# Recurrent linear attention and an MLP mixer on one core: u of batches 2 and 3 transposed by DMA instead of TensorE

## The chip, the core and the metric

The kernel runs on one NeuronCore of a Trainium2 chip. The core has five engines with instruction streams of their own: TensorE (PE; its weight loads, PEld, are listed apart) multiplies matrices into PSUM, eight banks of 128 x 512 float32; VectorE (DVE) and ScalarE (ACT) read PSUM and SBUF; GpSimd (POOL) works on SBUF; SyncE (SP) here issues DMAs. Sixteen DMA engines move data between HBM and SBUF. The metric is the time of one execution in microseconds of device time. Lower is better.

## The reference

Four batches, 8 heads, 768 time steps, head size 48. First a recurrence with a decaying state, then a mixer over time steps and over channels:

```python
for t in range(S):                                    # S = 768
    state = alpha[:, :, t, :, None] * state + einsum('bhd,bhe->bhde', k[:, :, t], v[:, :, t])
    y[:, :, t] = einsum('bhd,bhde->bhe', q[:, :, t], state)
x = y.transpose(0, 2, 1, 3).reshape(B, S, H * D)      # 4 x 768 x 384
h = relu(x^T @ w_tok1) @ w_tok2                       # over time: 768 -> 256 -> 768
u = x + h^T
out = u + relu(u @ w_ch1) @ w_ch2                     # over channels: 384 -> 1536 -> 384
```

Inputs and output are float32; the kernel multiplies in bfloat16 and sums in float32.

## The kernel before

A batch is cut into six chunks of 128 time steps; unit n is batch n // 6, chunk n % 6. The work of a batch has these stages, named as the program names its operations:

- Loads: alpha, k, q and v of a chunk, 192 KB each, float32, by SyncE into `in` buffers with eight slots (line 205). Batch 0 and the start of batch 1 load pairs of chunks, 384 KB.
- Attention of a chunk: `la` is the logarithm of alpha (ScalarE), `cum` its running sum over the chunk (one matmul of 384 columns and four of one column, lines 352 and 355), `ek` and `eq` its exponentials (ScalarE), `pkk` and `pkq` k and q scaled by them (mostly GpSimd, line 275), `tr` and `tp` their transposes through PSUM, `gt` and `gm` the products of keys and queries and their mask, `state`, `st` and `ss` the carried state, `y` the result, copied to the tile x as bfloat16.
- Token mixing: `tok1` (line 602), `ht` (its relu), then `tok2`, two matmuls a chunk (line 651), and `u`, an addition on VectorE that turns the tile x of a chunk into u in place (line 657).
- Transposing u: the channel matmuls need u with channels on the partitions. In `separate` (batches 1 to 3), for each half of a batch (three chunks), operation `utp` transposes the three x tiles by 18 small matmuls against the identity, two 64-row halves of each of nine 128 x 128 blocks, into two PSUM banks (`row_tiles`, line 289), and two operations `ut` copy the banks to the tile `ut` (line 669), one a 64-row half. Batch 0 (`mixed`) computes u transposed directly and keeps doing so.
- Channel mixing (`channel`): 24 `ch1` of three matmuls a batch, reading `ut` (line 691), each followed by `rt`, a relu out of PSUM into one of 24 `rt` tiles (line 589 on ScalarE, 591 on VectorE); then for each chunk three `ch2` parts of four matmuls (line 715), `o` (adds u, line 728) and `out`, a store of 192 KB by SyncE (line 731).

Nothing is scheduled at run time. The functions above only build a list of operations; `ORDER`, a text found by an offline planner, says in which order they are emitted, and each engine runs its own instructions in that order. An entry is an operation's number in the list; digits after a point are the PSUM banks that it gets; a letter A, D or P chooses ScalarE, VectorE or GpSimd where there is a choice; `f` and a bank is a filler, a matmul of zeros (line 792), of which there are 61, all ahead of the first ch1 of batch 0. The numbers in `costs` and the new `late` are what the planner reckoned with, in microseconds; the program does not read them. An instruction that must wait holds up all that stand behind it on its engine; this holds for SyncE's and ScalarE's DMA issues too.

In the order before, u of batch 2 is transposed at 107.9 us and that of batch 3 at 144.9 us of the profiled execution, between the last ch2 parts of the batch before and the first ch1 of its own; the attention of batch 3 is spread among the ch1 of batch 2.

Of the kernel before, what the change touches and what calls it, by code (L numbers as in the profile page):

```python
# [17 lines left out]
FUSE = 99  # L18
FETCH, BLOCK, AHEAD, ARRIVES = 193, 256, 449, (4.5, 30.0, 3.0)
# [6 lines left out]
0 1 f0 2 f0 f0 f0 f0 f0 3 f0 f0 f0 f0 f0 4 28 f0 29 f0 f0 30.0 5 31.1 32 f2 f2 38 6 f2 35 f2 33 f2 f2 f2 39 f2 34 f2  # L26
36 40 f2 43.2 41 7 f3 66 47.3 f4 65 48 44 49A 50D f4 67.4 46A 45D 68.5 69 f6 51.67 75 72 54.01 8 70 52 f3 f3 76 f3 73
f3 77 f3 80.3 78 f2 9 84.2 56 f6 85 105 81 71 f6 104 87D f6 f6 10 86A f6 f6 83D 106.6 82A 55 107.5 108 53 91.14 11 114
88.23 92 f0 42P 37A f0 f0 109 90 f0 58.07 115 89 57.13 60A 93 f2 116 12 f2 f2 59 f2 f2 f2 112 f2 111 63 61 117 14
123.2 64A f0 62 f0 124 74A 79P 119.0 110 16 120 125D 126A f4 94.41 122A 121D 18 96 127.57 97 130.36 95.20 128 113A  # L30
118P 100 132 98 102 133.4 99A 20 131 13P f5 103A 169.5 101 163.6 24 166.2 f3 15P 129 141.3 135 142.0 143 136 134.17
17P 137 139 145 138D 147 140A 144 146 259 148 150 149 151 19D 152 172.4 178.1 162A 161D 175.7 f0 173 176 174A 167 177D
260 164 168A 170 22D 21P 165A 179 f0 171A 23D f0 261 f0 180A f0 189.0 201.3 190A 195.4 262 202A 181.7 27D 25P 196A
185.2 26D 182A 153 193.6 186A 211.5 264 194D 223.1 263 212D 227.0 224A 265.3 228A 266.4 155 267 217.7 273 270 207.2
274 209.6 268 300 208D 218A 276 213.5 210D 215.1 214A 269 187.0 301 271 216A 203.4 188A 219.3 275 204A 302 225.2 220A
154D 199.7 272 226A 278.65 277 279 200A 303 221.1 280D 281A 156P 183.0 222A 282 283 184A 292.43 284D 285A 197.2 304
294 286.71 157 305 198D 289.05 205.6 287 306.4 288 206A 159 191.2 308 291 307.7 309 311 239.6 296 314 343 290 315
249.1 297 192D 293.54 344 312 319.37 298 295A 345 254.0 316 299A 234.2 158A 346 317 244.5 347 310 313 160D 240 318 348
245 351 241 349 320 352.4 242A 321D 246 322A 354 235 247D 353 350 358 236 356 243 323 362 324 237D 333.64 357 325A
326D 376.5 238 363.2 335 250 248 355 364 336 486 365 327.37 251 487 329 366 367 330.62 328 252A 488 255 332 368 256  # L40
339 369 359.73 331 257A 370.12 340 229.4 361A 360D 253 372D 371A 377 373.60 258 510 334.73 375 489 381.21 341 490 374
337 230 342A 378 382 338A 491 379.5 383 231 380A 492 384.0 232D 511.6 385A 493 513 388.3 512 516 233 386.2 389A 514
517 494 521 495 515 387D 522.7 390.1 496 523 398.5 391 524 394.4 526 396.0 399 392.6 395 400.3 527 535.2 393 518.17
401 497 402.54 528 519A 397 529.63 525 403A 553.1 404D 498 520A 536 405.05 530A 416.4 499 554 406A 440.7 407D 555 531A
500 417D 420.2 539 434.6 421D 441A 501 532.10 435A 550.53 534 422.4 502 430.2 551 546 423A 540.7 533 431A 452.6 558
552 442.0 541 537.5 453D 503 542 438.4 544 538D 559.2 439A 556.1 443D 504 560 543 412.3 545 557D 561 426.6 413D 505
432.7 564 427A 410.5 506 433A 446.4 562 411A 565 408.0 507 447A 563 572.1 577 450.2 409D 508 454.3 573 451A 547.67 574
455D 566.54 509 548A 578.0 549D 591.1 568A 567D 448.2 720 592 580 424.3 584 449D 579 588.76 583 721 425A 569.54 590
418.1 596 582 436.2 570 419A 414.0 571 437A 581 597.3 593 589 722 610.6 575.5 598 444.1 415D 599 601 723 576A 594.2
611 445A 481.4 595D 602 724 744 428.7 476.0 600 429A 725 603 604.35 612 585.61 605A 726 466.2 587D 586A 477 727 606A  # L50
482 728 607.73 751 615.16 609 483 729 755 616 471.5 608 478 617 613.3 730 479 472 614A 484 618.1 480 762 456.7 619D
473 485 773 622.6 731 474 732 620.0 623A 475 457 621A 733 458 734 634.3 459 630.4 735 628.1 635 632.5 631 624.6 780
460 626.0 629 461.7 625 792 736 627 462 737 633 463 636.34 738 464 639.16 637A 467 638D 640A 641D 465 468 799 774.0
469 745.5 775 793.7 656.4 746 778 747 756.3 470 650.6 795 739 757 749 684.1 651D 740 758 644.2 685D 776 748 662.5 794
760 645D 741 660.6 811 663D 657A 678.3 750 742 661D 787.0 769.1 679A 812.7 770 759 668.2 743 777 813 761 672.5 788 814
664.4 669A 673D 789 670.6 665A 666.3 779 671A 646.1 830 667D 682.0 798 647A 831.7 683A 806.2 781.54 797 832 807 763.63
833 752.10 765D 658.2 783A 835 754D 764A 674.7 753D 659D 782A 686.3 808 675D 800.40 687A 803.16 796 802D 816 784.25
801A 766.73 804 680.0 768 818 654.4 681A 836 767 648.1 655A 844.3 786 642.0 649A 817 771.7 785 822.41 643A 652.5 772A
805 834 837 790.2 824 815 653A 809.0 791A 823 838.76 810A 819.51 825.2 839D 820A 828.4 840D 676.0 821A 826 715.7 829D
827 677A 849.65 841.21 845 716 843 846 700.4 851 695.0 850 696 842 852.3 688.1 853D 847.5 689A 705.6 848D 697 854.2  # L60
698 699 717 855A 710.3 718 711 701 719 702 856.1 703 704 712 857A 690.5 713 858.0 714 868.2 859 862.7 860.4 869 864.1
863 866.3 691 861 867 692 865 706 693 873.02 694 870.74 874A 875D 707 871D 872A 910.3 708 894.1 911A 709 880.5 895A
908.2 881D 906.0 909A 912.7 907A 900.4 913A 876.6 901A 896.3 877A 918.1 897A 914.5 919D 904.2 915A 922.0 905D 902.7
923D 920.4 903A 898.6 921A 916.3 899A 888.1 917A 890.5 889A 884.2 891D 878.0 885A 886.7 879A 882.4 887A 892.6 883D
929.3 893A 939.1 930 931 940 932 944.5 933 945 946 934.2 947 941 948 924.0 942 925 943 926 935 927 936 928 949.7 937
950 938 951 954.4 955 952 956 953 957 958
# [12 lines left out]
class Graph:  # L79
# [5 lines left out]
    def add(self, name, costs, emit, reads=(), writes=(), prio=0, dma=None, new=(), tail=0.0, rows=False, loose=False, n=0, late=0.0):  # L85
        self.ops.append(Op(costs, emit, new))
        return self.ops[-1]
# [6 lines left out]
def kernel(  # L94
# [12 lines left out]
    nc = tc.nc  # L107
    B, H, S, D = q.shape
    C = 128
# [232 lines left out]
    def natural_front(n):  # L342
# [7 lines left out]
        def cum(e):  # L350
# [3 lines left out]
            for j in range(4):  # L354
                pe.matmul(ps[:, HD + j : HD + j + 1], lhsT=la[:, 2 * j : 2 * j + 2, :], rhs=ones_col,  # L355
                          start=True, stop=True, skip_group_check=True)
# [478 lines left out]
```

## Time and profile before

| | |
|---|---|
| median of 3 runs | 174.6 us (173.99 to 174.98) |
| the profiled execution's own time | 174.24 us |
| its span, first to last instruction | 172.5 us |
| granted TensorE clock | 1.0 |
| TensorE busy | 166.5 us (96%) |
| TensorE weight loads | 106.8 us |
| VectorE, ScalarE, GpSimd busy | 102.0, 96.0, 72.3 us |
| DMA | 30.20 MB, 175 GB/s over the span |

The profile is of one execution. Its page has the busy time of each engine, the span in 40 slices (a digit is the busy share in tenths), the chain of work that ended last, and groups of instructions by source line. Further views of the trace are used below: the busy time in stretches of the span (length, then busy time and count of TensorE, its weight loads, VectorE, ScalarE and GpSimd, then the granted clock, the DMA engines' share and GB/s), the list of who waited for whom (total, times, longest), the chain of waits in order of time (start, length, instruction), the timeline of an engine, and the instructions of one source line (duration least, median and greatest in ns, first and last start). Matmuls overlap, so their pitch is read from the chain, where each entry begins at the end of the one before, and not from their durations. A DMA's time to landing runs from its issue to its semaphore.

### The profile page before, as it was taken

How to read it: one execution, taken by the hardware profiler on the slowest of the kernel's cores; microseconds unless marked ns; L12 is line 12 of the kernel's file. 1: busy time of each engine (PE TensorE's matmuls, PEld its weight loads, DVE VectorE, ACT ScalarE, POOL GpSimd, SP SyncE). 2: the span in 40 equal slices, each digit the busy share in tenths (PEclk: the TensorE clock that was granted, in tenths of full speed). 3: DMA queues.
4: the chain of work that ended last, by engine and by line, in shares of the span. 5: the costliest groups of instructions: out<-in, count | busy, mean ns of one | idle time of the engine just before them, and what ended most of it. 6: DMA issues, size and time to landing. Idle time of an engine off the chain costs nothing.

```text
span 172.5 us, 5143 instructions
## 1 busy us (share of the span) xinstructions
PE 166.5 (96%) x2099; PEld 106.8 (62%) x2099; DVE 102.0 (59%) x212; ACT 96.0 (56%) x206; POOL 72.3 (42%) x114
## 2 busy tenths in 40 slices
PE   7999979999999999999999999999999999999993
PEld 3566656665666567566666665666676656656562
DVE  3159977544653597689593727495988248132231
ACT  2577552699865655497887231699771112865000
POOL 7252542319485782944877111499941000000000
PEclk9999999999999999999999999999999999999999
DMA  5999999999998999999999999995000221100133
GB/s 134 261 261 265 232 335 398 309 234 337 256 307 168 205 254 219 225 170 198 165 204 151 196 219 223 211 210 92 4 4 0 79 104 50 46 4 0 46 115 113
DMA packets 86150, 30.20 MB, mean 175 GB/s; under 512 B 79600, under 2 KB 85104, under 8 KB 86128
## 3 DMA queue, kind: packets, MB, share of 16 engines
q1 hardware_dynamic: 86128, 29.89, 75.2%
q8 instruction: 16, 0.26, 0.7%
q14 instruction: 6, 0.05, 0.1%
HBM read 25.17 MB, written 4.72 MB: 173 GB/s over the span
## 4 chain that ended last, share of the span: by engine, by line
PE 78%; DVE 6%; POOL 4%; DMA 3%; issue 3%; ACT 2%; SPq 1%; DVEq 0%; POOLq 0%
PE bank L691 27%; PE bank L715 23%; PE bank L289 4%; PE bank L651 3%; DMA ina<-in_alpha_dram 3%; PE bank L602 3%; DVE gm L309 2%; PE bank L387 2%; PE bank L338 2%; PE bank L423 2%; POOL pkk L275 2%; PE bank L521 1%; PE bank L411 1%; PE bank L352 1%; SPq L205 1%
## 5 line engine op out<-in xcount | busy, mean ns | idle before, releaser
L691 PE MATMUL bank<-ut,wc 128*128 128x384 bf16 x288 | 51.1, 326 | 0.0
L691 PEld LDWEIGHTS <-wc 128*128 128x128 bf16 x288 | 26.6, 98 | 16.5
L275 POOL TENSOR_TENSOR pkk<-ink,ek 128x384 bf16<-128x384 f32 x24 | 24.3, 1022 | 17.7 <-ACT ek L256 14.9
L715 PE MATMUL bank<-wc,rt 128*128 128x384 bf16 x144 | 26.5, 326 | 0.0
L715 PE MATMUL bank<-wc,rt_late 128*128 128x384 bf16 (+2 forms) x156 | 25.1, 314 | 0.0
L728 DVE TENSOR_TENSOR o<-bank,x 128x384 f32<-128x384 f32 (+2 forms) x19 | 10.1, 536 | 18.2 <-PE bank L715 18.2
L589 ACT ACTIVATE rt<-bank 128x384 bf16<-128x384 f32 x33 | 16.3, 494 | 7.4 <-PE bank L691 7.0
L282 POOL CAST vb<-inv 128x384 bf16<-128x384 f32 x21 | 10.5, 506 | 22.3 <-DMA inv<-in_v_dram 17.6
L715 PEld LDWEIGHTS <-rt_late 128*128 128x128 bf16 x156 | 14.4, 98 | 8.2
L275 POOL TENSOR_TENSOR pkq<-inq,eq 128x384 bf16<-128x384 f32 x18 | 17.9, 1003 | 2.8 <-ACT eq L258 2.8
L589 ACT ACTIVATE rt_late<-bank 128x384 bf16<-128x384 f32 x33 | 16.1, 495 | 5.3 <-PE bank L691 5.3
L309 DVE TENSOR_TENSOR gm<-bank,u 128x512 bf16<-128x512 f32 x28 | 17.3, 682 | 2.8 <-PE bank L387 2.6
L243 ACT ACTIVATE la<-ina 128x384 bf16<-128x384 f32 x24 | 12.1, 526 | 10.8 <-DMA ina<-in_alpha_dram 10.8
L715 PEld LDWEIGHTS <-rt 128*128 128x128 bf16 x144 | 13.2, 98 | 7.7
L792 PE MATMUL bank<-zeros 128*128 128x384 bf16 x61 | 15.1, 372 | 1.4 <-DVE la L192 1.2
L591 DVE TENSOR_SCALAR rt_late<-bank 128x384 bf16<-128x384 f32 x15 | 8.3, 554 | 10.0 <-PE bank L691 8.3
L309 DVE TENSOR_TENSOR gm<-bank,pmask 128x512 bf16<-128x512 f32 x20 | 12.7, 682 | 1.4 <-PE bank L521 1.3
L256 ACT ACTIVATE ek<-bank 128x384 f32<-128x384 f32 x24 | 11.4, 498 | 3.5 <-PE bank L355 2.0
L333 ACT CAST x<-bank 128x384 bf16<-128x384 f32 x16 | 7.3, 483 | 10.6 <-PE bank L338 9.4
L322 POOL TENSOR_TENSOR ss<-st,al 128x384 bf16<-128x384 f32 x12 | 10.0, 832 | 7.4 <-DVE st L319 5.4
L591 DVE TENSOR_SCALAR rt<-bank 128x384 bf16<-128x384 f32 x15 | 7.9, 554 | 5.3 <-PE bank L691 5.3
L297 ACT COPY tkq<-bank 128x512 bf16<-128x512 bf16 x17 | 9.3, 602 | 2.8 <-PE bank L289 2.7
(118 smaller groups left out, 237.3 us busy)
## 6 DMA issues: line engine op xcount, KB each, us to landing
out_dram<-o SPq DMA_DIRECT2D x23, 192.0 KB, 2.6
ina<-in_alpha_dram SPq DMA_DIRECT2D x14, 192.0 KB, 4.3
ink<-in_k_dram SPq DMA_DIRECT2D x14, 192.0 KB, 4.6
inq<-in_q_dram SPq DMA_DIRECT2D x14, 192.0 KB, 4.5
inv<-in_v_dram SPq DMA_DIRECT2D x14, 192.0 KB, 4.4
rt_late<-in_moe_w_ch_dram SPq DMA_DIRECT2D x2, 1152.0 KB, 10.1
rt_late<-in_moe_w_ch_dram SPq DMA_DIRECT2D x4, 576.0 KB, 7.1
ina<-in_alpha_dram SPq DMA_DIRECT2D x5, 384.0 KB, 6.3
```

Of the source, the lines that this page charges most:

```text
L243: g.add("la", {"ACT": 0.43}, lambda e: act.activation(la[:, :, 0:D], t, AF.Ln), key, [u["la"][1]], pr + 5)
L256: g.add("ek", {"ACT": 0.38}, lambda e: act.activation(ek, banks[bank.place][:, 0:HD], AF.Exp, scale=-1.0), [bank], [kek], pr + 4)
L275: lambda e, dst=dst, src=src, ex=ex: {"POOL": gps, "DVE": dve}[e].tensor_tensor(dst[:, :, 0:D], src, ex().rearrange("p (h d) -> p h d", h= ...
L282: lambda e: evict[e](vb, src), ksrc, [u["vb"][1]], pr + 4)
L309: g.add("gm", {"DVE": 0.60}, lambda e: dve.tensor_tensor(gm, banks[bank.place].rearrange("p (j t) -> p j t", j=4), wide(mask, [[0, 4], lis ...
L322: g.add("ss", {"POOL": 0.79}, lambda e: gps.tensor_tensor(ss, st.rearrange("p (h d) -> p h d", h=H), wide(al, [[1, 8], [0, D]]), ALU.mult) ...
L589: act.activation(dst, src, AF.Relu)
L591: dve.tensor_scalar_max(dst, src, 0.0)
L691: pe.matmul(banks[bank.place][:, 0:HD], lhsT=wc1[wp][:, kc, off : off + 128], rhs=ut_t[b % 2][:, kc, cs], start=(kc == 0), stop=(kc == NM ...
L715: pe.matmul(banks[bank.place][:, 0 : hi - lo], lhsT=rt_t[(b * NDC + mc) % NRT][:, i * 128 : i * 128 + 128], rhs=wc2[:, mc, lo:hi], start=( ...
L728: g.add("o", {"DVE": 0.09 + 0.38 * width}, lambda e, i=i, bank=bank, o=o, lo=lo, hi=hi: dve.tensor_tensor(o[:, lo:hi], banks[bank.place][: ...
L792: pe.matmul(banks[place][:, 0:HD], lhsT=zeros[:, 0:128], rhs=zeros, start=True, stop=True, skip_group_check=True)
```

## The change

For batches 2 and 3 the 18 transposing matmuls and two copies of each half are replaced by one DMA that ScalarE issues, which reads three x tiles of 128 x 384 and writes them transposed from SBUF to SBUF. For this the x tiles become slices of four larger tiles of three chunks, and `ut` gets the layout chunk, channel block, time, so that one half is one contiguous run on each partition. The copies and matmuls that write and read `ut` are rewritten for the layout, with the same sizes. Batch 1 is transposed as before. The two other options that the diff brings, `TRD` and `TOT`, are off. The loads are the same transfers as before.

The operation list is eight shorter, so operations behind those of batch 2 have new numbers, and the whole order was searched anew with the costs of the diff: 1.3 us of ScalarE for a transposing DMA, and its data 3.0 us later. It has 63 fillers, again all ahead of the first ch1.

```diff
+UTD, TRD, TOT = (2, 3), (), False
...
-    x_t = many("x", NX, [128, HD])
+    x_all = many("x", 4, [128, 3, HD])
+    x_t = [x_all[n // 3][:, n % 3, :] for n in range(NX)]
...
-    ut_t = many("ut", 2, [128, NM, S])
+    ut_t = many("ut", 2, [128, NCH, NM, C])
...
             ku = [("x", (n0 + i) % NX) for i in mine]
+            if b in UTD:
+                x = x_all[(n0 + mine[0]) % NX // 3]
+                g.add("utd", {"ACT": 1.3}, lambda e, x=x, cs=cs: nc.scalar.dma_start_transpose(
+                    ut[:, cs].rearrange("p i j t -> p (i j) t"), x.rearrange("p i d -> p (i d)")), ku,
+                    [("ut", b % 2, j, part, h) for j in range(NM) for h in range(2)], 1000 * b + 170, late=3.0)
+                continue
             tb = [Bank(), Bank()]
...
             for h in range(2):
                 g.add("ut", {"ACT": 0.50, "DVE": 0.43}, lambda e, tb=tb, h=h, cs=cs: evict[e](
-                    ut[:, :, cs].rearrange("p j (i t) -> p j i t", t=128)[:, :, :, 64 * h : 64 * h + 64],
+                    ut[:, cs, :, 64 * h : 64 * h + 64].rearrange("p i j t -> p j i t"),
...
                 pe.matmul(banks[bank.place][:, 0:HD], lhsT=wc1[wp][:, kc, off : off + 128],
-                              rhs=ut_t[b % 2][:, kc, cs], start=(kc == 0), stop=(kc == NM - 1),
+                              rhs=ut_t[b % 2][:, ti, kc, :], start=(kc == 0), stop=(kc == NM - 1),
```

Of the two orders, the stretch in which u of batch 2 is transposed. Before:

```
460 626.0 629 461.7 625 792 736 627 462 737 633 463 636.34 738 464 639.16 637A 467 638D 640A 641D 465 468 799 774.0
469 745.5 775 793.7 656.4 746 778 747 756.3 470 650.6 795 739 757 749 684.1 651D 740 758 644.2 685D 776 748 662.5 794
```

Here 636 and 639 are the `utp` of the two halves and 637, 638, 640, 641 their copies; 656.4 and 650.6 are the first ch1. After:

```
621A 769 471.4 729 469 628.6 634.0 470 629 626.1 624.3 635 630.2 730 627 472 731 625 473 631 636 776 732 632.6 474
461.0 633 788 462 637 463 477 475 464 478 458 479 795 741.1 459 789.3 743 752.2 770.4 742 460 744 674.6 746 753 465
666.0 754 675D 480 771 680.7 745 667D 790 644.5 733 681D 791 656.1 734 772 756 645D 668.2 807 657D 654.6 773 669A 757
```

The even numbers 624 to 634 are tok2 and the odd ones 625 to 635 the additions u; 636 and 637 the transposing DMAs of chunks 0 to 2 and 3 to 5; 461 to 463, 472, 473, 477, 478 and 458 ch2 parts of batch 1; 464, 469, 474, 479 and 459 its o; 470, 475, 460, 465 and 480 its stores; 741, 752, 770 and 789 cum of batch 3, with 742 and 743, 753 and 754, 771 and 772, 790 and 791 their ek and eq; 769, 788 and 807 la; 745, 746, 756 and 757 pkk and pkq; 776 and 795 vb, the cast of v; 729 to 734 loads of batch 3; 674, 666, 680, 644, 656, 668 and 654 ch1 of batch 2, of which 674 and 666 read the first half of u and 680 the second. For batch 3:

```
838 647A 711.4 847 661A 843.7 846 712 844A 848.6 706.3 849A 707 852.2 850.5 853A 701.0 851A 696.1 862.7 864.6 863
860.2 856.5 865 858.7 861 854.6 697 859 867 855 698 857 686.2 699 866 691.7 700 708 692 709 702 710 703 713 704 693
705 714 687 715 694 688 695 908.6 689 900.5 909A 690 882.1 901A 868.3 883A 890.0 869A 894.4 891A 902.7 895A 872.2 903A
```

Even numbers 854 to 864 are tok2, odd ones 855 to 865 the additions u, 867 and 866 the transposing DMAs of chunks 3 to 5 and 0 to 2; 697, 698, 686, 691, 708, 692, 702, 703, 713, 693, 687 and 688 ch2 parts of batch 2; 908, 900 and 882 the first ch1 of batch 3.

More of the change, by code (lines that the diff above doesn't have):

```diff
@@ L31 @@
[L31 to L35, printed above, removed]
@@ L83, in __init__, with add @@
         self.ops = []
-    def add(self, name, costs, emit, reads=(), writes=(), prio=0, dma=None, new=(), tail=0.0, rows=False, loose=False, n=0, late=0.0):
+    def add(self, name, costs, emit, reads=(), writes=(), prio=0, dma=None, new=(), tail=0.0, rows=False, loose=False, n=0, late=0.0, banks=(), gates=()):
         self.ops.append(Op(costs, emit, new))
@@ L353, in cum @@
                       skip_group_check=True)
[L354 removed]
+            for j in range(0 if TOT else 4):
                 pe.matmul(ps[:, HD + j : HD + j + 1], lhsT=la[:, 2 * j : 2 * j + 2, :], rhs=ones_col,
                           start=True, stop=True, skip_group_check=True)
[L358 to L359 removed]
+        g.add("cum", {"PE": 0.17 if TOT else 0.27}, cum, [kla], [bank], pr + 4, new=[bank], n=1 if TOT else 5)
+        s_exps(n, bank, 0 if TOT else 4, pr, n < NCH)
+        if TOT:
+            al, kal = u["al"] = al_t[n % NEX], ("al", n % NEX)
+            eq = eq_t[n % NEX]
+            if ci < NCH - 1:
+                g.add("ald", {"ACT": 0.13}, lambda e: [nc.scalar.dma_start(
+                    wide(al[64 * r : 64 * r + D, r : r + 1], [[2, 4]]),
+                    wide(eq[127:128, D * r : D * r + 1], [[1, D], [2 * D, 4]])) for r in range(2)],
+                    [("eq", n % NEX)], [kal], pr + 4, late=2.3)
     def natural_run(ns):
```

94 lines of the change are left out of this document (48 added, 46 removed).

## The prediction

> **What bounds the kernel now.** I read the page's span, busy lines and slices first, then the busy time by stage, then TensorE's waits, then the chain of waits around the two places where u of batches 2 and 3 is transposed.
>
> ```profile
> span 172.5 us, 5143 instructions
> PE   7999979999999999999999999999999999999993
> DMA  5999999999998999999999999995000221100133
> 0.00:33.00 33.00, 30.14 (x444) 19.63 (x445) 20.53 (x58) 17.93 (x39) 13.92 (x30) 1.00 1.07 276
> 75.00:107.90 32.90, 32.90 (x374) 20.78 (x374) 22.26 (x43) 19.63 (x43) 15.06 (x23) 1.00 1.08 193
> 107.90:110.70 2.80, 2.80 (x61) 2.03 (x61) 1.84 (x4) 1.56 (x3) 0.51 (x1) 1.00 1.03 217
> 110.70:144.90 34.20, 34.20 (x416) 22.23 (x415) 23.81 (x46) 17.51 (x40) 16.69 (x24) 1.00 0.30 71
> 146.30:158.00 11.70, 11.70 (x74) 7.05 (x72) 3.71 (x7) 8.51 (x18) 0.00 (x0) 1.00 0.05 19
> 158.00:169.80 11.80, 11.74 (x85) 7.61 (x82) 3.43 (x8) 0.49 (x1) 0.00 (x0) 1.00 0.23 83
> 169.80:172.50 2.70, 0.00 (x0) 0.00 (x0) 0.27 (x1) 0.00 (x0) 0.00 (x0) 1.00 0.23 74
> PE bank L651 <- DVE ht L591: 0.2, 1, 0.2
> ```
>
> In the stage rows the first pair is the stage, then its length and the busy time of TensorE, its weight loads, VectorE, ScalarE and GpSimd, the granted clock, the DMA share and GB/s. From 75 us to 169.8 us TensorE is busy for the whole of every stage but 0.06 us. The last row above is the only wait of TensorE from 33 us to the end that the list of waits has: 0.2 us. The end is TensorE's work in sequence plus a tail of 2.7 us with no matmul. Until the 28th slice the DMA engines are full as well, by the loads of all four batches. So there are two questions: how much TensorE work goes, and whether anything new makes TensorE wait.
>
> **The change, part by part: the work removed.** The chain of waits shows TensorE's pitch, since each entry ends where the next begins. (Start, length, instruction, count.)
>
> ```profile
> 104.05 1.95 PE bank L651 x12
> 106.00 1.95 PE bank L715 x12
> 107.94 0.63 PE bank L289 x36
> 108.58 1.41 PE bank L715 x8
> 110.14 0.08 PE bank L355 x4
> 110.22 0.18 PE bank L352
> ...
> 141.03 1.95 PE bank L651 x12
> 142.98 1.95 PE bank L715 x12
> 144.93 0.63 PE bank L289 x36
> 145.56 0.76 PE bank L715 x4
> 146.31 11.70 PE bank L691 x72
> L669 ACT COPY ut<-bank x6: 639/644/682, 73.8 to 145.9; 128x576 bf16<-128x576 bf16 x6
> L669 DVE COPY ut<-bank x6: 446/448/459, 73.9 to 145.7; 128x576 bf16<-128x576 bf16 x6
> ```
>
> The two L289 entries are the transposes of u, 36 of them for each batch. 0.63 us each, 1.26 us in all, on the path that sets the end. They go, and nothing on TensorE takes their place: the new order has as many matmuls of every other kind, and two more fillers (63 for 61), which all stand ahead of the first ch1, where the first stage row shows 33.0 - 30.14 = 2.86 us of idle TensorE that they take from; I cost them at nothing, and at 2 x 0.16 us if that idle time is gone.
>
> Eight copies out of PSUM go as well: two a part, of 0.64 us on ScalarE and 0.45 us on VectorE, in all 4 x (0.64 + 0.45) = 4.4 us. Neither engine bounds a stage (17.51 and 23.81 of 34.2 us), so this is worth nothing by itself. The new layout of u and the merged x tiles leave every matmul at the same size and its rows contiguous runs of 128 numbers; nothing.
>
> **The work added.** Four transposing DMAs of 128 x 1152 bf16, 288 KB each, issued by ScalarE. The trace has no such DMA. The planner's costs in the diff say 1.3 us of ScalarE and the landing 3.0 us later, 4.3 us in all; that is the change's own claim. The nearest rows are the stores from SBUF and the loads, first in the full stretch, then in the quiet one.
>
> ```profile
> L205 SPq DMA_DIRECT2D inq<-in_q_dram x7: 592/924/2031, 84.8 to 114.3; - x7
> DMA to landing us min/median/max: 3.1/4.3/5.9
> L731 SPq DMA_DIRECT2D out_dram<-o x6: 385/796/1267, 98.9 to 111.1; - x6
> DMA to landing us min/median/max: 3.3/4.0/4.7
> L731 SPq DMA_DIRECT2D out_dram<-o x13: 332/332/357, 135.1 to 170.1; - x13
> out_dram<-o SPq DMA_DIRECT2D x23, 192.0 KB, 2.6
> out_dram<-o SPq DMA_DIRECT2D x1, 128.0 KB, 1.7
> out_dram<-o SPq DMA_DIRECT2D x1, 64.0 KB, 1.5
> DMA to landing us min/median/max: 1.5/1.9/1.9
> 104.00:108.00 4.00, 4.00 (x33) 2.28 (x32) 3.36 (x8) 0.52 (x1) 0.51 (x1) 1.00 1.12 223
> 144.00:148.00 4.00, 4.00 (x58) 2.47 (x57) 2.39 (x6) 2.16 (x4) 0.00 (x0) 1.00 0.19 69
> ```
>
> Lower end: in the quiet stretch 64 KB land in 1.5, 192 KB in 1.9 us, 0.2 us for every 64 KB more; 288 KB would land in 1.9 + 0.3 = 2.2 us. Upper end: the slowest load of 192 KB in the full stretch took 5.9 us, and 5.9 x 1.5 = 8.9 us if all of it grows with size. A load there stands behind some four of its own queue; a transpose on ScalarE's queue does not, but shares the 16 engines. I take 4.8 us for batch 2: the loads' median of 4.3 and 0.5 us for the additional 96 KB (half of the 1 us by which loads land after each other there: 4 landings in a median of 4.3 us). For batch 3, where the engines are at 0.19, I take the diff's 4.3.
>
> The row with DMA share 1.12 is SyncE's queue alone. The Trainium skill, page "DMA: Bandwidth & Descriptors", section "Issuing engines are not separate DMA queues", says that DMAs of any issuing engine run on the same 16 DMA engines and interleave, so a second issuer saves issue time only. No run so far shows two queues at work. By that rule batch 2's transposes get a share of engines that are already full and go toward the 8.9 us end, at which the sum below becomes 176.8 us; without it they go toward 2.2 us, and the sum stays.
>
> **The slack.** Batch 2, from the new order, t = 0 at its first tok2. VectorE's additions, which the transposes read:
>
> ```profile
> 104.56 2.87 DVE L657 TENSOR_TENSOR x<-bank,x 128x384 bf16<-128x384 f32 x6
> 141.39 2.88 DVE L657 TENSOR_TENSOR x<-bank,x 128x384 bf16<-128x384 f32 x6 [0.42 <-PE bank L651]
> 105.55 0.52 ACT L243 ACTIVATE la<-ina 128x384 bf16<-128x384 f32 x1 [2.27 <-DMA ina<-in_alpha_dram]
> ```
>
> The first one begins 141.39 - 141.03 = 0.36 us after the first tok2, they follow each other at (2.88 - 0.55) / 5 = 0.47 us and last 0.55 us. Transpose 636 needs the first four: 0.36 + 3 x 0.47 + 0.55 = 2.3 us. Transpose 637 needs the sixth, which stands behind one o on VectorE: 4.1 us; on ScalarE it stands behind 636 (2.3 + 1.3) and the la of op 788 (0.5), also 4.1 us. TensorE has between t = 0 and the first ch1 six tok2 of two matmuls, eight ch2 parts of four and four cum: 44 matmuls at 1.95 / 12 = 0.1625 us and 4 x (0.18 + 0.08), 8.2 us. That ch1 reads 636: slack 8.2 - 2.3 = 5.9 us. The third ch1 reads 637, 6 x 0.1625 later: slack 9.2 - 4.1 = 5.1 us. Against 4.8 us: no wait, with 0.3 us to spare. Batch 3 has twelve ch2 parts there, 60 matmuls, 9.75 us: 867 issues at 1.8, 866 at 3.2 us, slack 6.5 us and more against 4.3: no wait.
>
> What is queued behind a waiting transpose on ScalarE: the la of chunk 3 and then the eq and ek of batch 3, of which the first eq waits for cum at 7.2 us, so 1.3 us of holding is covered. SyncE's out 475 stands behind an o, out 460 behind ch2 458, so loads 733 to 739 begin about when ch1 does, some 3 us later than now against TensorE; they feed chunks 4 and 5 of batch 3, and each is used 5 to 6 us of TensorE work after its place in the order, against a median of 4.3 us to land. That gap also lets the DMA engines run empty behind the first transpose.
>
> **Sum:** 174.24 us (the profiled execution: span 172.5 and 1.74 around it) - 1.26 + 0.2 for imperfect placing (the one wait that the old order has after 33 us) = 173.2 us. The median of the runs shown is 0.36 us above that execution; so 173.2 to 173.5, and I say 173.3. 0.5%, about what a measurement of this kernel can tell from no change, is 0.87 us.
>
> **Rivals.** *Late landing in batch 2, slower.* The first ch1 of batch 2 waits for the DMA's semaphore in place of the PSUM copy. For: DMA share 1.12, issue-to-landing up to 5.9 us. Against: the pause in SyncE's loads. Every microsecond above 5.1 is a microsecond of TensorE. It eats the gain at 5.1 + 1.3 = 6.4 us and is slower by more than 0.5% from 7.2 us. At 8.0 us: 174.24 - 1.26 + 2.9 = 175.9 us; at 8.9 us 176.8 us.
>
> *ScalarE held longer, no change.* SyncE's own issue takes 0.33 us in the quiet stretch and 0.92, at most 2.03 us, in the full one. If 636 holds ScalarE by 1.7 us more (2.03 - 0.33), 637 issues at 2.3 + 3.0 + 0.5 = 5.8 us and lands at 10.6 against 9.2 us: a wait of 1.4 us, 174.4 us. Against: the holding may fall into time in which ScalarE idles, as in the 2.27 us before the la above.
>
> *A wait elsewhere in the rewritten order, no change or a little faster.* GpSimd works through batch 3's products from 110.89 us, 0.9 us after the first cum, to 125.2 us without a break:
>
> ```profile
> 110.89 1.96 POOL L275 TENSOR_TENSOR pkk<-ink,ek 128x384 bf16<-128x384 f32 x2 [0.27 <-ACT ek L256]
> 123.26 1.96 POOL L275 TENSOR_TENSOR pkq<-inq,eq 128x384 bf16<-128x384 f32 x2
> ```
>
> The new order has two ch1 (1.0 us) fewer between that cum and the transposes that read the last product. If the old order has no more than that to spare, 0.5 to 1 us comes back: 173.7 to 174.2 us.
>
> **How the numbers follow.** Forecast 0.50 (own range 172.5 to 173.7); late landing 0.27; ScalarE held 0.14; elsewhere 0.09. Faster by over 0.5%: the forecast, and 0.01 of the last. Same: 0.14 and 0.08. Slower: 0.27. The low end is the gain with no wait and 0.5 us of the start's 2.86 idle us won, 172.5; the high end 176.0 is the late landing at 8.0 us, which leaves about half of that case and a twentieth of the forecast outside.
>
> **What would show it.** Right: no L289 on x after batch 1; TensorE's wait list after 33 us without a ch1 that waits for a DMA; transposes of batch 2 landing within 5.1 us, of batch 3 within 6.5 us; a span of about 171.4. Wrong: a wait L691 <- DMA at batch 2's first or third ch1, or ScalarE issue instructions well over 1.3 us, or new waits at L289 or L387 on GpSimd's products.

## The result, and the profile after

The changed kernel takes 175.25 us in the median (20 runs, 173.94 to 176.38), the kernel before 174.13 us (20 runs beside it). The ratio is 1.0039, interval 1.0022 to 1.0056: slower by 0.4%, inside the 0.5% that I had called no change, but clear of 1 and not the way that I had forecast, which was 173.3 us. The ratio is not the quotient of the two medians, which lie 1.12 us (0.64%) apart; the runs of both kernels spread unevenly, and I go by the ratio. The same kernel on two other occasions gave 1.0107 (1.0060 to 1.0154, four runs) and 1.0024 (0.9989 to 1.0059, twelve runs). The profiled execution took 175.22 us, 0.98 us more than that of before.

From the page of the changed kernel: span, busy TensorE, and the two DMA queues (packets, MB, share of the 16 engines). Its ch1 stands in line 712 (691 before), ch2 in 736 (715), tok2 in 666 (651), the transposing DMA in 682.

```profile
span 173.5 us, 5003 instructions
PE 165.6 (95%) x2029; PEld 105.5 (61%) x2029; DVE 96.9 (56%) x202; ACT 96.9 (56%) x208; POOL 72.7 (42%) x114
q1 hardware_dynamic: 86128, 29.89, 74.2%
q10 hardware_dynamic: 4736, 1.18, 3.9%
```

The second queue, q10, is ScalarE's: 1.18 MB, four transposes. VectorE lost its copies (102.0 to 96.9 us), and TensorE is busy for 0.9 us less. Yet the span is longer. Busy time by stage, in the columns of the stage rows above; the cuts are the first ch1 of batch 1, the first tok2 of batch 2, a moment inside the stall that follows, the first tok2 and the first ch1 of batch 3, and the end of the last matmul:

```profile
75.14:102.48 27.34, 27.23 (x332) 17.33 (x330) 17.80 (x35) 19.05 (x42) 14.46 (x22) 1.00 1.04 181
102.48:112.30 9.82, 9.34 (x72) 5.58 (x69) 6.15 (x13) 2.70 (x8) 2.35 (x5) 1.00 1.18 234
112.30:137.06 24.76, 24.04 (x344) 15.94 (x345) 16.89 (x33) 16.20 (x36) 15.31 (x22) 1.00 0.37 79
137.06:146.85 9.79, 9.79 (x62) 5.86 (x60) 5.67 (x11) 0.00 (x0) 0.00 (x0) 1.00 0.57 131
170.45:173.50 3.05, 0.00 (x0) 0.00 (x0) 0.29 (x1) 0.00 (x0) 0.00 (x0) 0.87 0.21 68
```

TensorE now idles for 0.48 + 0.72 = 1.2 us around 112.3 us, where it had been busy throughout. Around batch 3's transposes (fourth row) it does not idle. The tail without a matmul is 3.05 us. TensorE's waits after 33 us, the three longest (total, times, longest):

```profile
PE bank L712 <- DMA ut<-x: 1.2, 1, 1.2
PE bank L438 <- DVE gm L316: 0.4, 1, 0.4
PE bank L290 <- POOL pkk L276: 0.4, 1, 0.4
```

ScalarE's timeline (start, length) gives the two transposes of batch 2, the chain of waits what the end hung on, and the rows of line 682 all four:

```profile
104.99 1.40 ACTq L682 DMA_TRANSPOSE ut<-x  x1
106.66 2.42 ACTq L682 DMA_TRANSPOSE ut<-x  x1
110.13 0.49 ACT L259 ACTIVATE eq<-bank 128x388 f32<-128x388 f32 x1 [3.11 <-PE bank L362]
```

```profile
105.89 0.77 PE bank L736 x5
106.66 6.31 DMA ut<-x
112.97 0.05 issue
113.02 2.61 PE bank L712 x15
```

```profile
L682 ACTq DMA_TRANSPOSE ut<-x x4: 1306/1365/2424, 105.0 to 140.6; - x4
DMA to landing us min/median/max: 3.5/5.0/6.3
```

The second transpose was issued at 106.66 us and landed 6.31 us later. The ch1 that reads it had nothing to do from 111.82 to 113.02 us. The first landed in 5.55 us, and those of batch 3 in 3.45 and 4.44 us.

In this table the landings are those of batch 2's two transposes, from issue, and the wait is TensorE's on `ut`; the tail runs from the last matmul's end to the end of the span. Ratios are to the kernel before, run beside each.

| run | median us | ratio, 95% interval | span | landings b2 | wait | tail |
|---|---|---|---|---|---|---|
| before | 174.13 | 1 | 172.5 | - | - | 2.79 |
| after | 175.25 | 1.0039 (1.0022-1.0056) | 173.5 | 5.6, 6.3 | 1.2 | 3.05 |
| e1_layout | 174.11 | 0.9997 (0.9975-1.0018) | 172.5 | - | - | 2.80 |
| e2_swap | 174.16 | 0.9990 (0.9961-1.0020) | 171.5 | 4.9, 6.4 | 0 | 3.05 |
| e3_quiet | 173.30 | 0.9966 (0.9936-0.9995) | 171.6 | 3.6, 4.0 | 0 | 3.05 |
| e4_b2_pe | 174.97 | 1.0043 (1.0020-1.0066) | 173.2 | - | 0 | 2.90 |
| e5_mid_swap | 174.47 | 1.0015 (0.9986-1.0044) | 172.6 | 5.8, 5.3 | 0 | 3.05 |
| e6_b3_only | 176.42 | 1.0117 (1.0068-1.0166) | 173.7 | - | 0 | 2.90 |
| h_start | 174.21 | 1.0003 (0.9971-1.0035) | 172.0 | - | - | 2.80 |
| e7_sync | 174.28 | 0.9982 (0.9951-1.0014) | 173.2 | 4.7, 3.8 | 1.6 | 3.04 |
| e8_warm | 175.32 | 1.0051 (1.0016-1.0085) | 175.2 | 6.7, 5.8 | 0.9 | 2.99 |
| e2_again | 173.82 | 0.9964 (0.9928-1.0000) | 173.8 | 6.5, 6.3 | 0.7 | 3.04 |
| e9_swap_sync | 173.54 | 0.9948 (0.9925-0.9970) | 172.0 | 4.4, 3.6 | 0 | 3.05 |
| e10_order_pe | 174.46 | 1.0024 (1.0005-1.0042) | 172.6 | - | - | 2.87 |
| e9_again | 173.42 | 0.9944 (0.9925-0.9963) | 171.8 | 4.7, 3.6 | 0 | 3.05 |
| e11_mid_sync | 174.07 | 0.9995 (0.9979-1.0011) | 172.2 | 4.6, 3.6 | 0 | 3.06 |
| after_again | 176.18 | 1.0107 (1.0060-1.0154) | 173.9 | 6.1, 6.1 | 1.0 | 3.05 |
| after_third | 174.91 | 1.0024 (0.9989-1.0059) | 174.1 | 5.3, 6.3 | 1.2 | 3.05 |
| f2_sync | 174.33 | 1.0007 (0.9987-1.0027) | 173.2 | 4.6, 3.6 | 1.0 | 3.04 |
| f3_swap | 173.34 | 0.9950 (0.9922-0.9977) | 171.4 | 5.9, 6.4 | 0 | 3.05 |

The profiled executions of e8_warm and e2_again were slow ones, over 1.5% above the fastest run of their kernel, which the ratios leave out. A profile is one execution, and the new order's runs lie up to 3 us apart, so a verdict goes by the ratio and a profile by what waits for what.

### The profile page after: what moved, and what is told of

Same layout as the page of the kernel before. It is cut to its first block, busy times and chain, and to the rows that moved or that the text cites. A ratio compares the mean times of both kernels' runs of the same rounds, so it can differ in the third digit from the quotient of the medians.

```text
span 173.5 us, 5003 instructions
## 1 busy us (share of the span) xinstructions
PE 165.6 (95%) x2029; PEld 105.5 (61%) x2029; DVE 96.9 (56%) x202; ACT 96.9 (56%) x208; POOL 72.7 (42%) x114
## 3 DMA queue, kind: packets, MB, share of 16 engines
q10 hardware_dynamic: 4736, 1.18, 3.9%
## 4 chain that ended last, share of the span: by engine, by line
PE 65%; DMA 12%; SPq 8%; POOL 6%; ACT 4%; issue 2%; DVE 2%; DVEq 0%; ACTq 0%; POOLq 0%
PE bank L736 21%; PE bank L712 19%; DMA ina<-in_alpha_dram 9%; SPq L206 8%; DMA ut<-x 4%; PE bank L813 3%; PE bank L666 2%; PE bank L617 2%; POOL pkk L276 2%; POOL pkq L276 2%; PE bank L402 2%; PE bank L345 2%; PE bank L290 2%; ACT la L244 2%; PE bank L536 1%
## 5 line engine op out<-in xcount | busy, mean ns | idle before, releaser
L276 POOL TENSOR_TENSOR pkk<-ink,ek 128x384 bf16<-128x384 f32 x24 | 23.7, 996 | 15.9 <-ACT ek L257 12.9
L604 ACT ACTIVATE rt_late<-bank 128x384 bf16<-128x384 f32 x39 | 18.9, 492 | 13.5 <-PE bank L712 13.4
L283 POOL CAST vb<-inv 128x384 bf16<-128x384 f32 x21 | 11.0, 529 | 18.9 <-DMA inv<-in_v_dram 18.9
L813 PE MATMUL bank<-zeros 128*128 128x384 bf16 x63 | 14.5, 369 | 1.2 <-DVE la L193 1.2
L672 DVE TENSOR_TENSOR x<-bank,x 128x384 bf16<-128x384 f32 x18 | 8.7, 550 | 6.5 <-PE bank L666 6.5
L340 ACT CAST x<-bank 128x384 bf16<-128x384 f32 x13 | 6.0, 479 | 9.8 <-PE bank L345 7.3
L259 ACT ACTIVATE eq<-bank 128x388 f32<-128x388 f32 (+2 forms) x18 | 8.9, 505 | 4.0 <-PE bank L362 3.4
```

What stands on the lines that cost most here:

```text
L276: lambda e, dst=dst, src=src, ex=ex: {"POOL": gps, "DVE": dve}[e].tensor_tensor(dst[:, :, 0:D], src, ex().rearrange("p (h d) -> p h d", h= ...
L283: lambda e: evict[e](vb, src), ksrc, [u["vb"][1]], pr + 4)
L604: act.activation(dst, src, AF.Relu)
L813: pe.matmul(banks[place][:, 0:HD], lhsT=zeros[:, 0:128], rhs=zeros, start=True, stop=True, skip_group_check=True)
```

## The experiments

My theory after the result: the rival of the late landing came true, and without it the gain would show. The rivals to that: the layout, the rewritten order, or the transposing DMAs themselves cost it.

**The layout alone** (e1_layout).

```diff
-UTD, TRD, TOT = (2, 3), (), False
+UTD, TRD, TOT = (), (), False
...
-0 1 f0 2 f0 f0 f0 f0 f0 3 f0 f0 f0 f0 f0 4 28 f0 29 f0 f0 31.0 5 30.1 38 f2 f2 32 40 f2 6 f2 39 f2 f2 f2 33 f2 41 35
+0 1 f0 2 f0 f0 f0 f0 f0 3 f0 f0 f0 f0 f0 4 28 f0 29 f0 f0 30.0 5 31.1 32 f2 f2 38 6 f2 35 f2 33 f2 f2 f2 39 f2 34 f2
...
```

> The order of the kernel before, word for word, with the new layout of u and the x tiles merged to four, and all transposes on TensorE: only the data layout of the change. If the late landing in batch 2 or the rewritten order costs the time, this equals the kernel before within 0.3% (0.5 us). If the layout costs something (matmul rows in three runs, coarser dependences between x tiles), it is slower by 0.5 us or more and TensorE's wait list after 33 us grows beyond 0.2 us.

0.9997, and the first ch1 of batches 1, 2 and 3 at 74.80, 110.61 and 146.15 us, within 0.01 us of before. The layout costs nothing that shows.

**Later use of the second half** (e2_swap, e2_again, f3_swap). Four pairs of ch1 of batch 2 change places with their relus, so that six ch1 instead of two read the first transpose before one reads the second. Nothing else differs from the changed kernel.

```diff
-666.0 754 675D 480 771 680.7 745 667D 790 644.5 733 681D 791 656.1 734 772 756 645D 668.2 807 657D 654.6 773 669A 757
+666.0 754 675D 480 771 654.7 745 667D 790 642.5 733 655D 791 650.1 734 772 756 643D 670.2 807 651D 680.6 773 671A 757
...
```

> The changed kernel with four pairs of ch1 of batch 2 exchanged, so that the first six read the first half of u and the seventh is the first to read the second half: its slack grows by 4 x 0.49 = 1.95 us, from 5.1 to 7.0 us against the 6.3 us that the transpose took. If the late second transpose of batch 2 is what cost 1.2 us, that wait is gone and the time falls by 1.0 to 1.3 us against the changed kernel, to about the kernel before or 0.3 us under it. If the loss lies in the order ahead of batch 2's transposes, the time stays within 0.4 us of the changed kernel's, and the wait is only exchanged for another.

> The kernel of e2_swap once more, for a second profile: its runs lay between 173.2 and 175.3 us, and its profile was of the fastest. Theory (the spread comes from the loads at 33 to 75 us and a wait on la behind them): in a slower execution the first ch1 of batch 1 is late by most of the difference, the span behind it is 96.5 us as in the first profile. Rival (the spread comes from the transposes): a wait on ut, or landings above 6.4 us, and the loss lies behind 100 us.

> The kernel of e2_swap beside after_third. Theory (the wait of the third ch1 is what the exchange takes away): 0.5 to 0.7% below after_third, 0.995 to 0.999 against before. Rival (the exchange is worth less than the wait, the first ch1 then waits for the first transpose): 0.3% or less below after_third.

Three occasions: 0.9990, 0.9964, 0.9950; the first interval includes 1, the second ends at it, the third lies below it. Beside after_third on the same chip f3_swap is faster by 174.91 - 173.34 = 1.57 us in the median, and by 1.0024 - 0.9950 = 0.74%, 1.3 us, in the ratios, against a wait of 1.2 us taken away. TensorE's waits after 33 us in f3_swap, and its transposing DMAs:

```profile
PE bank L438 <- DVE gm L316: 0.4, 1, 0.4
PE bank L290 <- POOL pkk L276: 0.4, 1, 0.4
PE bank L557 <- POOL vb L283: 0.2, 1, 0.2
L682 ACTq DMA_TRANSPOSE ut<-x x4: 1305/1347/2496, 104.0 to 138.5; - x4
DMA to landing us min/median/max: 3.5/5.2/6.4
```

No wait for `ut`, although its second transpose took 6.37 us to land. So the wait in batch 2 is what took the gain away, and where the late landing is covered the change gains. The spans of single profiles differ by more than the wait: the first tok2 of batch 2 stands at 101.45 us in f3_swap, at 102.48 us in the changed kernel and at 103.11 us in after_third, behind the same instructions. That part of the difference isn't the exchange's.

The cover is not ample: in after_again, where the first transpose landed after 6.08 us, the first ch1 itself waited 0.3 us, and in e2_again's profile 0.7 us, after 6.47 us. Of the 2.3 us by which e2_again's profiled execution is longer than e2_swap's, 0.28 us were there at the first ch1 of batch 1, 1.04 us at the first tok2 of batch 2 and 1.86 us at its first ch1. So for that execution neither theory was right alone: part was lost ahead of the transposes, part to the late landing.

**Without the loads** (e3_quiet). It leaves out the 16 loads of batch 3's chunks 2 to 5, of which some are issued just before and beside the transposes of batch 2.

```diff
+SKIP = {str(n) for n in range(724, 740)}
...
+            if what in SKIP:
+                continue
```

> The changed kernel without the sixteen loads of chunks 2 to 5 of batch 3, which then work on what the buffers hold of batch 2: the DMA engines have nothing but stores beside the transposes of batch 2. If sharing the engines with the loads makes these transposes late, they land as those of batch 3 did (3.5 and 4.4 us), ScalarE is held 1.3 to 1.4 us by each, and TensorE's wait for ut is gone. If the second transpose is slow because it follows the first on ScalarE's queue, it still takes 5.5 us or more and holds ScalarE 2.4 us.

The same transposes in the same order, with busy time from 104 to 113 us: first the changed kernel, then e3_quiet with its rows of the transposing DMA.

```profile
104.00:113.00 9.00, 7.82 (x62) 4.65 (x60) 5.17 (x11) 3.39 (x9) 3.05 (x6) 1.00 1.21 253
```

```profile
104.00:113.00 9.00, 9.00 (x71) 5.57 (x70) 5.74 (x12) 3.91 (x10) 2.81 (x4) 1.00 0.64 154
```

```profile
L683 ACTq DMA_TRANSPOSE ut<-x x4: 1304/1333/1648, 104.5 to 138.7; - x4
DMA to landing us min/median/max: 3.6/3.9/4.4
```

With the DMA share at 0.64 instead of 1.21 the two land in 3.60 and 4.04 us instead of 5.55 and 6.31, and there is no wait. It is the sharing with the loads that makes them late here. By the rule of the Trainium skill that the prediction cited (page "DMA: Bandwidth & Descriptors", section "Issuing engines are not separate DMA queues"), the DMAs of both issuers interleave on the same 16 engines; the trace agrees, with 2.0 and 2.3 us more beside the loads.

**Batch 2 on TensorE, batch 3 by DMA** (e4_b2_pe, e6_b3_only). e4 keeps the changed kernel's order, e6 has the order of before up to the tok1 of batch 3.

```diff
-UTD, TRD, TOT = (2, 3), (), False
+UTD, TRD, TOT = (3,), (), False
...
```

> The changed kernel's order with batch 2 transposed on TensorE again (36 small matmuls and four copies at the places of the two DMAs); batch 3 by DMA. If the wait for the late transpose is the cost, this removes 1.2 us and adds 0.63 us: 0.6 us faster than the changed kernel. If the DMA transposes of batch 2 cost nothing and the order is to blame, it is 0.63 us slower than the changed kernel.

> The order of before up to the tok1 of batch 3 (136 us), batch 2 transposed by TensorE, then the end of after's order with batch 3 transposed by DMA. All loads are done by then. Theory (the DMA is worth its removed transposes where it stands beside nothing): transposes land in 3.4 to 4.4 us, no wait, 0.63 us less TensorE, 0.2 us of longer tail: 173.6 to 173.8 us, ratio 0.997. Rival (e4's 4.9 and 5.4 us were no chance: a transposing DMA alone is slow too, and the order of after costs time even here): landings of 5 us and more, 174.2 us or above, ratio 1.000 or more.

Both missed, for reasons of their own making: TensorE's waits after 33 us in e4, then in e6.

```profile
PE bank L666 <- ACT ut L690: 0.7, 1, 0.7
PE bank L438 <- DVE gm L316: 0.4, 1, 0.4
```

```profile
PE bank L403 <- DVE st L327: 1.1, 1, 1.1
PE bank L439 <- DVE gm L317: 0.5, 1, 0.5
```

In e4 a tok2 waits for a bank that I gave to the transposes; in e6 the join of the two orders makes TensorE wait 1.1 us for the state at 128 us. As times they say nothing on the change. What stays: batch 3's transposes met no ch1 that waited, although they landed in 4.9 and 5.4 us (e4) and 4.7 us (e6). That is later than the 3.45 and 4.44 us of batch 3 in the changed kernel and than e3_quiet's, and beside stores alone. So the loads are not the only thing that can make the first two transposing DMAs of a program late; no run here shows what else does.

**The start of the new order** (h_start: after's order up to the first ch1 of batch 0, then before's; no DMA transposes).

```diff
-UTD, TRD, TOT = (2, 3), (), False
+UTD, TRD, TOT = (), (), False
...
```

> After's order up to the first ch1 of batch 0, then before's order; no DMA transposes. In after that ch1 came 0.7 us earlier, and the lead was gone by the first ch1 of batch 1. Theory (33 to 75 us goes at the pace of the loads, so an earlier start is worth nothing): first ch1 of batch 0 at 32.2, of batch 1 at 74.8 us, 174.2 us, ratio 1.000. Rival (the lead is lost only by after's own order in 33 to 75 us): first ch1 of batch 1 at 74.1, 173.5 us, ratio 0.996.

The ratio is 1.0003 (0.9971 to 1.0035): nothing that shows. The profiled execution (173.74 us) kept 0.5 us of the lead, with the first ch1 of batch 1 at 74.30 us, so a single execution can show the rival's picture.

**The new order alone** (e10_order_pe: after's order, with batches 2 and 3 transposed by TensorE two or three ch2 parts ahead of their first ch1).

```diff
-UTD, TRD, TOT = (2, 3), (), False
+UTD, TRD, TOT = (), (), False
...
-461.0 633 788 462 637 463 477 475 464 478 458 479 795 741.1 459 789.3 743 752.2 770.4 742 460 744 674.6 746 753 465
...
+633 792 462 463 477 475 464 636.13 639.24 637A 638D 640A 641D 478 458 479 799 745.1 459 793.3 747 756.2 774.4 746 460
...
```

> After's order, with the transposes of batches 2 and 3 on TensorE again (36 matmuls and four copies each, two or three ch2 parts ahead of the first ch1); no transposing DMA. What differs from before is the order alone. Theory (the new order itself loses 0.3 us against the loads in 33 to 75 us and 0.4 us in 80 to 100 us, and its runs spread): first ch1 of batch 1 at 75.1 us, 174.9 us, ratio 1.004, runs over 1.5 us. Rival (the order costs nothing, all of after's loss is the DMA): 174.2 us, ratio 1.000. The tail tells one more thing: 2.8 us if the transposing DMAs make it longer, 3.05 us if the order does.

1.0024 (1.0005 to 1.0042): the order by itself costs 0.24% of 174.1, 0.4 us (0.1 to 0.7), between the two expectations. In the profile (174.31 us) the last matmul ends at 169.74 us, as in before, so I can't say where in a median run these 0.4 us lie. The tail is 2.87 us, not 3.05.

**The order of before ahead of the transposes** (e5_mid_swap, e11_mid_sync): before's order for its first 620 entries, then the rest of e2_swap's; in e11 SyncE issues the transposes.

```diff
-                g.add("utd", {"ACT": 1.3}, lambda e, x=x, cs=cs: nc.scalar.dma_start_transpose(
+                g.add("utd", {"ACT": 1.3}, lambda e, x=x, cs=cs: nc.sync.dma_start_transpose(
```

> The order of before up to 96 us of its TensorE work (through the ch1, ch2 and attention that stand ahead of the tok2 of batch 2), from there the order of after with the four exchanges of e2; DMA for batches 2 and 3. Theory one (after's rewritten order ahead of batch 2 loses time against the loads, in 33 to 99 us): without it the whole gain of 1.26 us shows, less about 0.25 us of longer tail: 173.2 us, ratio 0.994, first ch1 of batch 1 at 74.8 us as in before, runs close together. Theory two (what e2's median lost is the transposes against the loads of batch 3, after 99 us): like e2, median 174.0 to 174.3, ratio 0.999, runs from 173.2 to 175.3, and TensorE's waits between 100 and 120 us show it.

> e5_mid_swap with the transposes issued by SyncE. Theory (SyncE's queue helps in any order): landings of batch 2 below 4.7 us, no wait on ut, 0.3 us or more below e5's ratio of 1.0015. Rival (only the swapped order of after gains by it, e5's loss being waits on GpSimd's products at 90 to 92 us): the same 1.0015, landings short, excess again at 90 to 92 us.

No wait on `ut` in either, and still 1.0015 and 0.9995: theory one falls. Not much waits in e5's list after 33 us:

```profile
PE bank L666 <- DVE ht L606: 0.2, 1, 0.2
PE bank L290 <- POOL pkq L276: 0.2, 1, 0.2
```

but its matmuls stand apart by 0.78 us more than before's from 80 to 100 us, most of it at 90 to 92 us, at the seam of the two orders, and e11's by as much. An order joined from two good ones isn't a good one; these runs leave open which half of the new order costs its 0.4 us.

**The issuing queue** (e7_sync: the changed kernel with the line of e11's diff; f2_sync the same again; e9_swap_sync and e9_again: e2_swap with it; after_again and after_third: the changed kernel).

> After's order, but the four transposes are issued by SyncE, at the same places of the order, in place of ScalarE. Theory (a transposing DMA is late in batch 2 because the loads share the engines with it, whoever issues it): landings of batch 2 again 4.9 to 6.4 us from issue, the wait of TensorE on ut stays at about 1 us; the tail from the last matmul to the end of the span goes back from 3.05 to 2.8 us, since there is one DMA queue fewer to wait for; SyncE's loads behind the first transpose begin up to 2 us later, so a wait for la may come in the attention of batch 3: 174.7 to 175.5 us. Rival (the second queue is what makes it slow): landings of 3.5 to 4.5 us, no wait on ut, 173.6 to 173.9 us.

> The kernel of e7_sync beside after_third. Theory (the issuing queue matters: with SyncE's, the load behind the transpose waits 2.7 us and the engines are less full): 0.4% or more below after_third. Rival (in e7's profile the wait on ut was 1.6 us, as long as in after, so the queue is worth nothing in this order): the same ratio as after_third within 0.2%.

> e2_swap with the transposes issued by SyncE. Theory (the tail of 0.26 us is the second DMA queue, and loads behind the transposes have slack): tail 2.8 us, no wait on ut, 0.2 us below e2_swap of the same call, 173.0 us in its fastest run. Rival (loads of batch 3 behind a transpose that waits for u come too late): waits on la behind 110 us, 174.5 us and more.

> The kernel of e9_swap_sync on another occasion. Theory (transposes from SyncE's queue land in 3.3 to 4.7 us because the loads behind them wait for the issue, so the swapped order has slack): no wait on ut, 173.5 us, ratio 0.995. Rival (the first result was luck of the loads): 174.2 us, ratio 1.000.

> The changed kernel once more, beside the others, for a second profile of it. Theory: landing of batch 2's second transpose 5.5 to 6.5 us from its issue, a wait on ut of 0.5 to 1.5 us, ratio 1.004. If the wait were the whole cause, the span less the wait would be before's less 1.0 us.

> The changed kernel, on one chip with f2_sync and f3_swap. Its ratios so far were 1.004 and 1.011. Theory: between them, 1.003 to 1.008, with a wait on ut of 1.0 to 1.3 us in the profile.

SyncE's timeline in the changed kernel, then in e9_again:

```profile
104.92 0.65 SPq L206 DMA_DIRECT2D inv<-in_v_dram  x1
105.67 1.83 SPq L206 DMA_DIRECT2D ina<-in_alpha_dram  x1
107.59 4.15 SPq L752 DMA_DIRECT2D out_dram<-o  x4
```

```profile
104.40 1.01 SPq L206 DMA_DIRECT2D inv<-in_v_dram  x1
105.50 2.79 SPq L682 DMA_TRANSPOSE ut<-x  x1
108.39 0.53 SPq L206 DMA_DIRECT2D ina<-in_alpha_dram  x1
109.02 1.89 SPq L682 DMA_TRANSPOSE ut<-x  x1
```

From SyncE a transpose of batch 2 lands in 3.6 to 4.7 us from its issue, where I had expected 4.9 to 6.4 us, but it is issued later, since the second stands behind the first's 2.8 us and a load. Counted from the first tok2 of batch 2, the second lands after 10.5 us in after and after 11.1 us (e7) and 10.3 us (f2) from SyncE. So in the unswapped order the wait stays, in f2_sync:

```profile
PE bank L712 <- DMA ut<-x: 1.0, 1, 1.0
PE bank L438 <- DVE gm L316: 0.4, 1, 0.4
```

and f2_sync's ratio is 0.17% below that of after_third, with intervals that overlap: beside each other the two can't be told apart. Over all occasions the two ratios from SyncE, 0.9982 and 1.0007, lie below the three of the changed kernel, 1.0024 to 1.0107, so a gain of a few tenths of a per cent is neither shown nor ruled out. The shorter tail that I expected fell: 3.04 us. With the exchange, SyncE's version gave 0.9948 and 0.9944, 172.8 to 174.6 us in 18 runs. It beats both kernels, as e2_swap does on its third occasion; on the one occasion that had both, e9 and e2 don't differ by more than their intervals (0.9948 and 0.9964).

after_again's theory held for the wait but not for the ratio, 1.0107 in four runs. Taking the wait alone off its span gives 172.9 us, not the 171.5 us of before's span less 1.0. Of the 1.4 us between them, two waits for la ahead of the transposes are 0.6 us and the tail 0.26 us; the other 0.5 us isn't accounted for. after_third's 1.0024 lay just below the 1.003 that I expected, with the wait as expected. Why the ratios on three occasions lie between 1.0024 and 1.0107, I can't say; the three profiles reach the first tok2 of batch 2 at 102.48, 102.92 and 103.11 us, so some of the spread lies ahead of the transposes.

**A transposing DMA issued earlier** (e8_warm: two small ones of 32 KB, at 94.1 and 98.0 us).

```diff
+            if item == "w":
+                nc.scalar.dma_start_transpose(ut_t[0][:, 0, 0, :], x_all[2][:, 0, 0:128])
+                continue
...
-432.6 419A 720 612 604.37 433A 585.04 605D 466.2 600 606A 721 603 586D 587A 456.5 740 722 607.16 615.37 609 481.0 723
+432.6 419A 720 612 604.37 433A 585.04 605D 466.2 600 606A 721 603 586D 587A 456.5 740 w w 722 607.16 615.37 609 481.0 723
```

> After, with two more transposing DMAs on ScalarE's queue at about 94 us, where ScalarE waits for a load: 128 x 128 of an x tile of batch 1 to a part of ut that is written over later, 32 KB each. In every run so far the second transposing DMA of the program held ScalarE 2.4 to 2.8 us (1.65 without the loads), whether it was one of batch 2 beside loads or one of batch 3 beside stores, and the third and fourth 1.3 us. Theory (being the second in the program is what makes it hold ScalarE long): the four of the kernel hold 1.3 to 1.4 us each, the second of batch 2 lands 1.1 us earlier, the wait on ut falls from 1.2 to 0.3 us or less: 174.2 to 174.4 us. Rival (the loads make it hold long): 2.4 us again, wait 1.2 us, 175.2 us.

```profile
L682 ACTq DMA_TRANSPOSE ut<-x x4: 1260/1352/1496, 106.3 to 142.3; - x4
DMA to landing us min/median/max: 3.3/5.1/6.7
```

The long hold of the second transpose is gone, 1.36 us for 2.42, but it began 2.7 us behind the first here, not 1.7, and this is one execution, of 176.92 us, so its cause isn't settled. The time did not fall, 1.0051: the transposes still land after 6.7 and 5.8 us. Nor does a longer hold go with a later landing elsewhere: the second transpose held ScalarE for 1.82 us and landed after 6.10 us in after_again, and for 2.45 and 5.25 us in e5_mid_swap.

## Why the prediction was right or wrong

**The step that failed: the landing time in batch 2.** The prediction took 4.8 us, the loads' median of 4.3 and half of the usual increment for the 96 KB more, "no wait, with 0.3 us to spare". Measured were 5.55 and 6.31 us, 6.08 and 6.10, 5.32 and 6.32 in the three profiles of the changed kernel. All else of the slack came out: the two issues 2.35 and 4.0 us after the first tok2 in the chain of waits (2.3 and 4.1 forecast), the first ch1 110.69 - 102.48 = 8.2 us after it (8.2). So the price rule of the rival held to the tenth: 6.31 - 5.1 = 1.2 us, the measured wait. That rival had 0.27 and the forecast 0.50. By its own sum the wait only eats the gain, 174.24 - 1.26 + 1.2 = 174.2 us, and the change is called slower from a landing of 7.2 us; that the kernel came out slower is due to the terms below that were too small, and in part not accounted for.

The error was to read the pause of SyncE's loads as an empty DMA. SyncE does pause from 107.6 to 111.8 us for stores, as foreseen, but the loads issued up to 105.67 us are then still in flight; the last took 6.6 us to land. The rows of the three loads issued from 104 to 107 us, and the changed kernel between the issue and the landing of the second transpose, with a DMA share of 1.23:

```profile
L206 SPq DMA_DIRECT2D ina<-in_alpha_dram x1: 1827/1827/1827, 105.7 to 105.7; - x1
DMA to landing us min/median/max: 4.2/5.4/6.6
106.66:112.97 6.31, 5.16 (x46) 3.04 (x43) 2.72 (x5) 3.20 (x9) 2.52 (x4) 1.00 1.23 260
```

The share of 1.12 before spoke for the upper end, 8.9 us; I took a value from the lower half of 2.2 to 8.9. The rule of the Trainium skill that the prediction cited spoke for the upper end too.

**The work removed, 1.26 us: right.** From batch 1's first ch1 to the last matmul e10_order_pe needs 169.74 - 74.80 = 94.94 us and f3_swap, the same order but for the exchange and the transposes, 168.35 - 74.56 = 93.79, 1.15 us less.

**Layout, fillers, copies at nothing: right as far as shown.** e1_layout shows the first. The new start brings the first ch1 of batch 0 forward by 0.7 us, and h_start's ratio shows no gain from that. No run takes the copies alone away; VectorE lost 5.1 us of work and bounds no stage.

**Batch 3: right.** 3.45 and 4.44 us against 4.3 taken, no wait.

**ScalarE held longer: half right, and harmless.** The second transpose held it for 2.42 us. What follows, the eq at 110.13 us, waited for TensorE's cum.

**Forgotten, or too small in the sum.** The sum had 0.2 us for imperfect placing. The tail grew by 0.26 us: 2.79 us before, 2.87 in e10, 2.90 with two transposing DMAs, 2.99 to 3.06 with four or more. So 0.08 us goes with the new order and 0.18 us with the four DMAs, not with ScalarE's queue, as I thought until e7. The order itself costs 0.4 us. Together that gives -1.26 + 1.2 (wait) + 0.4 (order) + 0.2 (tail beyond e10's) = +0.5 us; the first ratio says +0.7 (0.4 to 1.0) us, the medians 1.12 us, so up to 0.6 us isn't accounted for. The third rival named GpSimd's product train for such a loss. Its sign did appear, a new wait of 0.4 us on pkk, but at 74 us and not among batch 3's products, and it is 0.4 us in the changed kernel, e10 and f3_swap alike, so it isn't the cause of the wait on `ut`.

f3_swap, where the wait is gone, takes 173.34 us, the forecast's time; in part that is luck, since order and tail cost 0.6 us where the sum had 0.2. The mechanism was right. One duration, 1.5 us too small, took away the gain, and two small terms, with a rest that isn't accounted for, made a loss of it.

## What to carry to other kernels

A DMA in place of compute moves the question from engine time to landing time, and that must be taken from the stretch where it will run, beside what is in flight then: here 3.6 and 4.0 us without the loads and 5.3 to 6.3 with them. If the margin is less than that spread, first put more work between the issue and its first reader: exchanging four pairs of ch1 was worth more than changing the issuing engine (0.9950 and 1.0007 on the same occasion, with intervals apart). Check the price rule of the rival as carefully as the forecast, for here it gave the wait to the tenth. And price a rewritten order by a run of its own: it cost 0.4 us, a third of the work removed.

## What the runs showed of the hardware

A transposing DMA of 128 x 1152 bf16 from SBUF to SBUF held ScalarE for 1.30 to 1.36 us as the third or fourth of the program (1.50 us as the third in e8_warm, behind two small ones), and for 1.33 to 1.65 us as the first. The second held it for 1.82 to 2.82 us in nine profiles of ten (1.65 us in e3_quiet), whether loads ran beside it (2.42 us in the changed kernel) or, in e4 and e6, where it is one of batch 3, only stores (2.67 and 2.82 us). In e8_warm, whose second was a small one, none held it longer than 1.50 us. I had not expected that the place in the program counts, and no run here explains it. On SyncE's queue the first held for 2.55 to 2.79 us and the second for 1.64 to 1.93 us; loads of that queue held up to 1.83 us there, so that may be its backlog.

The other surprise is the tail: with the new order's end it is 2.87 us without a transposing DMA, 2.90 us with two and 3.04 to 3.06 us with four, whichever engine issues them (2.99 us with the six of e8_warm), though the last of them lands 28 us before the end in the changed kernel. No run here explains it.
